# Gram pieces taken out of the fused attention block, chunks given earliest times, and a new written-out order, in a gated-feed-forward kernel with a recurrent attention in front

## The chip, the cores and the metric

One core of one Trainium2 chip runs the whole program. The metric is device time in microseconds (us), the median of three runs. "PE" is the matrix engine, whose weight loads are listed apart as "PEld"; DVE is the vector engine, ACT the scalar engine, POOL the GpSimd engine, SP the queue that issues the transfers.

## The reference

A recurrent attention with a 48x48 state for each of 4 x 8 heads runs over 768 tokens, and its output goes through a gated feed-forward layer:

```python
for t in range(S):                       # 768 tokens
    kt, vt, bt = (k_n[:, :, t], v[:, :, t], beta[:, :, t, None])
    y[:, :, t] = np.einsum('bhd,bhde->bhe', q[:, :, t], state)
    v_old = np.einsum('bhde,bhd->bhe', state, kt)
    state = state + bt[:, :, :, None] * np.einsum('bhd,bhe->bhde', kt, vt - v_old)
...
x = y.transpose(0, 2, 1, 3).reshape(3072, 384)
out = ((x @ w_a) * (x @ w_b)) @ w_out    # w_a, w_b: 384 x 1536, w_out: 1536 x 384
```

## The kernel before

**Attention.** The 768 tokens are cut into 24 chunks of 32, and the chunks into six groups of four (`GROUPS`). Inside a chunk the recurrence is a small triangular system. For each group, `prep(g)` makes the Gram products of its four chunks (keys with keys and keys with queries, one PE piece a chunk) and DVE multiplies them by beta and a mask; `solve(g)` inverts the triangular systems by forward steps on DVE, 31 pairs of instructions for groups 2 to 5. Then `steps(g)` goes through the chunks in order, each with these PE pieces: **Yk** (keys and queries times the state, 32 calls), **U** (the solved update, 32 calls), **S** (the state gets the update, 32 calls, into the bank `S_ps`), **out** (the chunk's own part of the output, 32 calls). A piece of 32 small fp32 calls is issued without a break. From group 2 on (`more`), the **Gram** piece of the next group's chunk, S and out were one block of 96 calls, under one `plan.group()`.

**Feed-forward.** Two chunks make 128 x 2 rows of x, a "sub" of 256 tokens; there are 12 subs and 12 slices of 128 of the hidden width, so 144 units. A unit (`moe`) has 18 fp16 matmuls of 256 columns (here **D**, two runs of nine, with the weights `wh` split in a high and a low half), an ACT copy, a DVE product, an ACT cast, a DVE difference, and two units later (`LAG`) six matmuls of 384 columns with `wo` (here **O**, two runs of three). A unit of a sub needs the outputs of both its chunks.

**What sets the order.** All instructions are recorded first (`Plan.add`), and a planner writes the order of every engine down: `order()` runs `pack()` forward and backward over the recorded pieces. `pack()` is a list scheduler with a table of durations (`price`), delays between engines (`late`), six PSUM banks, a model of PE's clock, and `fetch()`, which counts PE instructions in blocks of 256 and puts a piece later when its block would not be there yet. `boost()` and `BOOST` add urgency by stream. Before, `order()` made up to six rounds (`PASSES`) and kept the one whose planned end was earliest. Until 60 us (`UNTIL`) the planner fills PE's idle time with dummy matmuls on a tile of ones (printed with the line of `issue()`, here 477), so that the clock stays up. At run time nothing of the planned times is left: each engine goes through its list in order and waits for semaphores.

The names `b_3_71` and `xn` are the transposed inverse of a group; `at`, `tt`, `f`, `u` are the small operands of out, U, U and S; `sh` is the copy of the state for Yk; `ghl` is the operand of O. All calls are issued from one helper line, 486.

Of the kernel before, what the change touches and what calls it, by code (L numbers as in the profile page):

```python
# [26 lines left out]
P = 128  # L27
KR = 112
GROUPS = [list(range(i, i + 4)) for i in range(0, NCH, 4)]
NG = len(GROUPS)  # L30
# [5 lines left out]
BOOST = {"first": 9e4, "prep0": 9e4, "solve0": 9e4, "steps0": 9e4, "w0": 7e4, "w1": 7e4, "w2": 6e4, "w3": 6e4, "w4": 6e4, "w5": 6e4, "prep1": 4e4, "solve1": 4e4, "steps1": 4e4, "moe": 1e5}  # L36
# [10 lines left out]
LAG = 2  # L47
LEAD = 4
# [3 lines left out]
class Op:  # L52
    __slots__ = ("eng", "calls", "dur", "move", "rd", "wr", "deps", "pri", "at", "end", "tag", "stream", "banks", "cold", "use", "words")

    def __init__(self, eng):
        self.eng, self.calls, self.dur, self.move = eng, [], 0.0, 0.0
        self.cold, self.use, self.words = 0.0, 0.0, 0
        self.rd, self.wr, self.deps, self.tag, self.banks = {}, {}, set(), "", set()


class Plan:
# [6 lines left out]
    def __init__(self, nc):  # L68
        self.nc = nc
        self.ops = []  # L70
        self.open = None
        self.stream = "first"
        self.masks = {}
        self.pool = []
        self.lease = {}
        self.leases = 0
        self.behind = set()

# [114 lines left out]
    def add(self, eng, fn, name, args, kw):  # L193
# [3 lines left out]
        if self.open is not None and self.open and self.open[-1].eng == eng:  # L197
            op = self.open[-1]
        else:
            op = Op(eng)  # L200
            kind = self.stream + ("_pe" if self.stream == "moe" and eng == "PE" else "")
            op.pri = len(self.ops) - URGENCY.get(kind, URGENCY.get(kind.rstrip("0123456789"), 0))
            op.deps, self.behind = self.behind, set()
            self.ops.append(op)
            op.tag, op.stream = name, self.stream
            if self.open is not None:
                self.open.append(op)
# [63 lines left out]
    def pack(self, pri, back=False):  # L271
# [10 lines left out]
        pos, come = self.BEGIN, [0.0, 0.0]  # L282
        kept = 0 if back else 1
# [5 lines left out]
        while len(done) < n:  # L289
# [23 lines left out]
            while can[e] and i is None:  # L313
                i = heapq.heappop(can[e])[1]
                if ops[i].words and not back:
                    slip = self.fetch(t, ops[i].words, ops[i].dur if warm else ops[i].cold, pos, come, dma)[0]
                    if slip > 1.0:
                        slow.setdefault(i, t)
                        heapq.heappush(wait[e], (t + slip, i))
                        i = None  # L320
                        continue
                need = [] if back else [b for b in ops[i].banks if b not in held]
                if need:
                    at_ = sorted((self.clear(ends, i), k) for k, ends in vacant)
                    if len(at_) < len(need):
                        blocked.append(i)
                        i = None
                    elif at_[len(need) - 1][0] > t:
                        heapq.heappush(wait[e], (at_[len(need) - 1][0], i))
                        i = None  # L330
                    else:
                        for b, (_, k) in zip(need, at_):
                            held[b] = [k, self.users[b], {}]
                        vacant = [x for x in vacant if x[0] not in {k for _, k in at_[: len(need)]}]
# [14 lines left out]
            if e == "PE" and not back:  # L349

                if kept:
# [12 lines left out]
                    while True:  # L364
# [9 lines left out]
                        fill[i][k] += 1  # L374
                _, pos, come = self.fetch(t, o.words, o.dur if warm else o.cold, pos, come, dma)
# [29 lines left out]
            for k, late in nxt[i]:  # L405
                ready[k] = max(ready[k], end + late)
                left[k] -= 1
                if not left[k]:
                    heapq.heappush(wait[ops[k].eng], (ready[k], k))
# [3 lines left out]
    LOADED = (3500.0, 4300.0)  # L413
# [17 lines left out]
    PASSES = 6  # L431

    def order(self):
# [16 lines left out]
        pri, best = [o.pri - boost(o) - 1e12 * (o.stream == 'load') for o in ops], None  # L450
        for _ in range(self.PASSES):
            found = self.pack(pri)
            if found is None:
                break
            at, stop, done, total, bind = found
            if best is None or total < best[0]:
                best = (total, at, stop, done, bind)
            _, stop, _, total, _ = self.pack([-t for t in stop], True)
            pri = [k - 1e12 if o.stream == 'load' else total - t - boost(o) for k, (o, t) in enumerate(zip(ops, stop))]
        for o, o.at, o.end in zip(ops, best[1], best[2]):  # L460
            pass
        self.bind, self.fill = best[4]
        return best[3]
# [26 lines left out]
def tile_kernel(ctx, tc, kqt, kn, vn, begin, w, out):  # L490
# [176 lines left out]
    def tok(h4):  # L667
        return slice(32 * h4, 32 * h4 + 32)
# [26 lines left out]

    def target(c, what):
# [21 lines left out]

    grams, rest = {}, []

    def gram(c):
        rw = raw(c)
        ga = grams[c] = att()
        plan.behind = set(ready if c > 3 else ())
        with plan.group():
            gram_mm(c)
        return ga

    def gram_mm(c):
        rw = raw(c)  # L730
        ga = grams[c].rearrange("p (q n) -> p q n", n=64)
        for q, h4, a, _ in heads():
            T.matmul(
                ga[tok(h4), q, :],
                rw[feat(h4), a, h4 % 2],
                pair(rw[feat(h4), a], h4 % 2),
                start=True,
                stop=True,
                skip_group_check=True,
            )  # L740

    def grammed(g, ci):
        c = GROUPS[g][ci]
        gnat, dc = gnats[g], dcs[g]
        ga = grams[c].rearrange("p (q n) -> p q n", n=64)
        if HALVES[g]:
            kks[c] = ttr()
            A.copy(kks[c], ga[:, :, 0:32])
        V.tensor_mul(
            gnat.rearrange("p k u -> p u k")[:, ci * 8 : ci * 8 + 8, :],  # L750
            ga[:, :, 0:32],
            dc[:, ci * 8 : ci * 8 + 8].unsqueeze(2).broadcast_to([P, 8, 32]),
        )
        ats[c] = atr()
        mask = partial(V.tensor_mul, ats[c], ga[:, :, 32:64], amask.unsqueeze(1).broadcast_to([P, 8, 32]))
        if c == 3:
            rest[:] = mask, {ga.tensor.name: plan.lease[ga.tensor.name]}
        else:
            mask()

    def prep(g):
# [25 lines left out]
        ready.append(len(plan.ops) - 1)  # L787
        gnat = b4().rearrange("p (a b) -> p a b", b=32)
        gnats[g] = gnat
        yield  # L790
        for ci, c in enumerate(chs):
            if g < 3:
                gram(c)
                grammed(g, ci)
            yield
# [125 lines left out]
    def steps(g):  # L921

        chs = GROUPS[g]
        for ci, c in enumerate(chs):
# [5 lines left out]
            else:  # L930
                sh = shr()
                A.copy(sh, S_ps[0:KR, :, 0:384])
                yp = [att(), att()]
                with plan.group():
# [29 lines left out]
            more = g > 1 and g + 1 < NG  # L964
            if more:
                nxt = GROUPS[g + 1][ci]
                grams[nxt] = att()
                lent = {grams[nxt].tensor.name: plan.lease[grams[nxt].tensor.name]}

            def update():  # L970
                for q, h4, a, cols in heads():
                    T.matmul(
                        S_ps[feat(h4), h4 // 2, cols],
                        k2[tok(h4), cols],
                        u[tok(h4), cols],
                        start=(first and q == 0),
                        stop=True,
                        skip_group_check=True,
                    )

            def output():
# [9 lines left out]

            if more:
                plan.behind = set(ready)
                with plan.group():
                    gram_mm(nxt)
                    update()
                    plan.lease.update(mine)
                    output()
            else:
                if not last:  # L1000
                    with plan.group():
                        update()
                plan.lease.update(mine)
                plan.behind = set() if last else {len(plan.ops) - 1}
                with plan.group():
                    output()
# [7 lines left out]
            if more:  # L1014
                plan.lease.update(lent)
                grammed(g + 1, ci)
# [156 lines left out]
    for g in range(1, NG):  # L1173
        n = len(GROUPS[g])
        if g < 2:
            merge((st[g], 3 * n), (moes, 4 * n), (pr[g + 1], 2 + len(GROUPS[g + 1])))
        elif g + 1 < NG:
            next(pr[g + 1])
            merge((st[g], 3 * n), (moes, 4 * n))
            merge((pr[g + 1], 2 + len(GROUPS[g + 1])), (moes, 2))  # L1180
        else:
            merge((st[g], 3 * n), (moes, 4 * n))
# [78 lines left out]
```

## Time and profile before

| what | value |
|---|---|
| median of 3 runs | 658.29 us (657.62 to 666.13) |
| profiled execution, device time | 656.6 us |
| its span, first to last instruction | 654.8 us |
| mean granted PE clock | 0.978 |
| PE busy | 625.1 us, 12208 matmuls |
| DVE busy | 405.0 us |
| ACT busy | 271.6 us |
| POOL busy | 46.0 us |
| transfers | 42.8 MB, mean 65 GB/s |

The device time is 1.8 us more than the span. A busy PE here means that a matmul is in flight: matmuls overlap, so the time that a piece costs is read from its start to the start of the next one. "issue" as the cause of a wait means that nothing which the profile shows (no semaphore, no transfer of data) held the engine back.

### The profile page before, as it was taken

Reading aid. Unit: us, or ns where it says so; the run is one execution under the profiler, and the core shown is the slowest. Engines: PE = TensorE matmul, PEld = TensorE weight load, DVE = VectorE, ACT = ScalarE, POOL = GpSimd, SP = SyncE. Lnnn points to the kernel's source line nnn. Section 1 sums busy time; section 2 is a strip of 40 time slices with the busy share of each in tenths; the row PEclk is TensorE's granted clock in tenths of the full one; section 3 lists DMA queues with packets and bytes.
Section 4 is the critical chain, followed back from the end, with each engine's and each line's share of the span. In section 5 each row is a group of like instructions: output and inputs, shape, how many; then the busy total and the mean of one; then the engine's idle time right before and its main releaser. Section 6 shows DMA issues by size and latency. Waiting matters only on the chain.

```text
span 654.8 us, 26975 instructions
## 1 busy us (share of the span) xinstructions
PE 625.1 (95%) x12208; PEld 534.1 (82%) x12208; DVE 405.0 (62%) x1059; ACT 271.6 (41%) x599; POOL 46.0 (7%) x134
## 2 busy tenths in 40 slices
PE   7998999899999999999989999989999999999997
PEld 6765888678888887888877788877788888888886
DVE  4976888679766994448964368844588442232222
ACT  3455763445534355332372223644224343232322
POOL 0111110111012110000020000100000000000000
PEclk7958999899999999999999999999999999999999
DMA  8655431342255300034000141000000000000000
GB/s 308 175 148 160 137 97 33 96 128 76 77 183 148 97 26 4 21 96 143 0 28 20 43 139 58 1 5 28 3 3 25 4 4 26 1 25 1 25 1 24
DMA packets 20754, 42.80 MB, mean 65 GB/s; under 512 B 2208, under 2 KB 5280, under 8 KB 20640
## 3 DMA queue, kind: packets, MB, share of 16 engines
q1 hardware_dynamic: 20640, 41.08, 20.6%
q8 instruction: 95, 1.56, 1.0%
q14 instruction: 19, 0.16, 0.1%
HBM read 36.36 MB, written 4.72 MB: 63 GB/s over the span
## 4 chain that ended last, share of the span: by engine, by line
PE 87%; DVE 6%; issue 4%; ACT 2%; DMA 1%; SPq 0%; DVEq 0%; ACTq 0%
PE bank L486 83%; PE S_ps L486 3%; DVE b L486 1%; DVE wh L486 1%; DVE tmp L486 1%; DMA rawb<-in_kqt 1%; ACT sqf L486 0%; PE bank L477 0%; DVE late L486 0%; ACT wh L486 0%; DVE ghl L486 0%; DVE f L486 0%; ACT tt L486 0%; DVE g L486 0%; ACT a L486 0%
## 5 line engine op out<-in xcount | busy, mean ns | idle before, releaser
L486 PEld LDWEIGHTS <-wh 128*128 128x128 f16 x2592 | 241.6, 98 | 53.0 <-issue 22.8
L486 PE MATMUL bank<-xb,wh 128*128 128x256 f16 x2160 | 259.5, 273 | 4.3 <-issue 2.7
L486 PE MATMUL bank<-wo,ghl 128*128 128x384 f32 x864 | 191.0, 354 | 0.1
L486 PEld LDWEIGHTS bank<-wo,ghl 128*128 128x128 f32 x864 | 144.7, 190 | 4.4 <-DVE ghl L486 0.5
L486 ACT COPY a<-bank 128x256 f32<-128x256 f32 x144 | 53.5, 372 | 210.8 <-PE bank L486 210.3
L486 DVE TENSOR_TENSOR g<-bank,a 128x256 f32<-128x256 f32 x144 | 61.0, 423 | 127.0 <-ACT a L486 124.0
L486 DVE TENSOR_TENSOR ghl<-g,ghl 128x256 fp32r<-128x256 f32 x144 | 62.1, 431 | 34.0 <-ACT ghl L486 31.9
L486 ACT CAST ghl<-g 128x256 fp32r<-128x256 f32 x144 | 58.1, 404 | 53.6 <-DVE g L486 52.7
L486 DVE TENSOR_TENSOR tmp<-b,b 128x31 f32<-128x31 f32 (+20 forms) x154 | 50.3, 327 | 3.2
L486 PE MATMUL bank<-late,wh 128*128 128x256 f16 x432 | 51.9, 273 | 0.0
L486 DVE TENSOR_TENSOR b<-b,tmp 128x31 f32<-128x31 f32 (+20 forms) x154 | 49.7, 323 | 3.3
L486 PE MATMUL bank<-u,at 32*32 32x48 f32 x1536 | 23.6, 203 | 10.1 <-issue 10.1
L486 PEld LDWEIGHTS bank<-u,at 32*32 32x32 f32 x1536 | 19.1, 105 | 15.1 <-issue 14.2
L486 DVE SCALAR_TENSOR_TENSOR y<-bank,sc,y 128x384 f32<-128x384 f32 x23 | 14.2, 616 | 25.1 <-ACT y L486 24.9
L486 ACT COPY sh<-S_ps 112x768 f32<-112x768 f32 x23 | 18.3, 798 | 22.9 <-PE S_ps L486 22.8
L486 PEld LDWEIGHTS bank<-rawb 48*32 48x32 f32 x1280 | 20.4, 114 | 7.7 <-issue 4.0
L486 PE MATMUL bank<-rawb 48*32 48x64 f32 x1280 | 23.2, 228 | 3.3 <-DMA rawb<-in_kqt 2.4
L486 PEld LDWEIGHTS bank<-sh,rawb 48*64 48x64 f32 x1216 | 19.7, 136 | 5.1 <-issue 3.4
L486 DVE TENSOR_TENSOR b<-bank,dc 128x256 f32<-128x256 f32 x24 | 14.3, 600 | 14.2 <-PE bank L486 13.5
L486 PEld LDWEIGHTS bank<-f,tt 32*32 32x32 f32 x1472 | 17.2, 105 | 6.5 <-issue 3.0
L486 PE MATMUL bank<-sh,rawb 48*64 48x48 f32 x1216 | 22.1, 222 | 0.0
L486 DVE TENSOR_TENSOR f<-vnb,bank 128x384 f32<-128x384 f32 x38 | 19.9, 549 | 3.1 <-PE bank L486 3.1
(123 smaller groups left out, 576.1 us busy)
## 6 DMA issues: line engine op xcount, KB each, us to landing
late<-in_w SPq DMA_DIRECT2D x40, 288.0 KB, 3.0
rawb<-in_kqt SPq DMA_DIRECT2D x32, 256.0 KB, 2.9
out<-late SPq DMA_DIRECT2D x24, 192.0 KB, 1.9
vnb<-in_vn SPq DMA_DIRECT2D x10, 384.0 KB, 3.6
kb<-in_kn SPq DMA_DIRECT2D x9, 384.0 KB, 3.5
wh<-in_w SPq DMA_DIRECT2D x8, 288.0 KB, 3.0
rawb<-in_kqt SPq DMA_DIRECT2D x2, 1024.0 KB, 7.1
late<-in_kqt SPq DMA_DIRECT2D x8, 256.0 KB, 2.7
```

What stands on the lines that cost most here:

```text
L486: fn(*(self.place(a, lease) for a in args), **{k: self.place(a, lease) for k, a in kw.items()})
```

## The change

Five things change.

1. The Gram piece of groups 3, 4 and 5 leaves the fused block. It is issued from `prep(g)`, as it was for groups 0 to 2, as a piece of its own; S and out are two pieces of 32 calls instead of parts of one of 96.
2. An operation can carry an earliest planned time (`hold`). The Yk piece of chunk c from 8 on gets 190 us + (c - 8) x 23 us; the Gram pieces get a time below zero, which holds nothing.
3. `fetch()` is asked three times after 60 us, with the count of PE instructions as planned and 14 fewer and more, and the latest answer counts. The two durations of a block's load go from 3500 and 4300 ns to 3700 and 4400.
4. The priorities come from one round and a fixed list of 38 random changes to them (`jitter`), and the forward pass is made once with the result.
5. The order in which the pieces are recorded for groups 2 to 5 changes (`merge`).

```diff
-    PASSES = 6
+    PASS = 1
+    SEEDS = (100008, 100012, 100025, ..., 103652)
...
+PACE = (190e3, 23e3)
+GRAM = (-1e6, 0)
...
+    LOADED = (3700.0, 4400.0)
+    SHIFTS = (-14, 14)
...
-                    slip = self.fetch(t, ops[i].words, ops[i].dur if warm else ops[i].cold, pos, come, dma)[0]
+                    slip = max(
+                        self.fetch(t, ops[i].words, ops[i].dur if warm else ops[i].cold, p, c, dma)[0]
+                        for p, c in [(pos, come)] + (more if t > self.UNTIL else [])
+                    )
...
-                    heapq.heappush(wait[ops[k].eng], (ready[k], k))
+                    heapq.heappush(wait[ops[k].eng], (max(ready[k], 0.0 if back else ops[k].hold), k))
...
+        for seed in self.SEEDS:
+            pri = jitter(pri, ops, seed)
+        best = self.pack(pri)
...
     def prep(g):
...
         for ci, c in enumerate(chs):
-            if g < 3:
-                gram(c)
-                grammed(g, ci)
+            rw = raw(c)
+            ga = att().rearrange("p (q n) -> p q n", n=64)
+            plan.behind = set(ready[-1:] if g > 2 else ready if g else ())
+            if g > 2:
+                plan.hold = pace(4 * g - 4) + GRAM[0] + ci * GRAM[1]
+            with plan.group():
+                for q, h4, a, _ in heads():
+                    T.matmul(ga[tok(h4), q, :], ...)
...
     def steps(g):
...
                 yp = [att(), att()]
+                if c > 7:
+                    plan.hold = pace(c)
                 with plan.group():
...
-            if more:
-                plan.behind = set(ready)
-                with plan.group():
-                    gram_mm(nxt)
-                    update()
-                    plan.lease.update(mine)
-                    output()
-            else:
-                if not last:
-                    with plan.group():
-                        update()
-                plan.lease.update(mine)
-                plan.behind = set() if last else {len(plan.ops) - 1}
-                with plan.group():
-                    output()
+            if not last:
+                with plan.group():
+                    for q, h4, a, cols in heads():
+                        T.matmul(S_ps[feat(h4), h4 // 2, cols], ...)
+            plan.lease.update(mine)
+            plan.behind = set() if last else {len(plan.ops) - 1}
+            with plan.group():
+                for q, h4, a, cols in heads():
+                    T.matmul(yp[h4 % 2][tok(h4 ^ 1), cols], ...)
...
-            next(pr[g + 1])
-            merge((st[g], 3 * n), (moes, 4 * n))
-            merge((pr[g + 1], 2 + len(GROUPS[g + 1])), (moes, 2))
+        todo = [(st[g], 4 * n), (moes, 4 * n)]
+        if g + 1 < NG:
+            todo.append((pr[g + 1], 2 + len(GROUPS[g + 1])))
+        merge(*todo)
```

What it moves is seen in the written-out order. First PE, at chunk 8, the first with a fused block. `rawb 32x64 x32` is the Gram piece, `S_ps<-u_74,kb` is S, the rows that alternate two banks with `u_74,at_77` are out, `xb,wh` is D. Before:

```order
L486 LDWEIGHTS wh
L486 MATMUL bank_64<-xb,wh 128x256
L486 MATMUL bank_66<-rawb 32x64 x32
L486 MATMUL S_ps<-u_74,kb 48x48 x32
L486 MATMUL bank_65<-u_74,at_77 32x48
L486 MATMUL bank_63<-u_74,at_77 32x48
```

The same place in the changed kernel:

```order
L515 MATMUL bank_65<-wo,ghl_100 128x384 x3
L515 MATMUL S_ps<-u_74,kb 48x48 x32
L515 LDWEIGHTS wh
L515 MATMUL bank_61<-xb,wh 128x256
...
L515 MATMUL bank_66<-rawb 32x64 x32
L515 MATMUL bank_63<-u_74,at_77 32x48
L515 MATMUL bank_64<-u_74,at_77 32x48
```

S now stands ahead of nine D matmuls, and the Gram piece and out behind them; at the other chunks of groups 2 to 4 the three pieces are parted in other ways.

Second PE, where the small products of group 1's solution begin (`tt_85` and `tt_86 32x16`, with `kb 128x256` and `xn 16x16` behind them). Before:

```order
L486 MATMUL bank_66<-wo,ghl_100 128x384 x3
L486 MATMUL bank_64<-b_3_71,tt_85 32x16 x32
L486 MATMUL bank_62<-b_3_71,tt_86 32x16 x32
L486 MATMUL bank_64<-b_3_71,kb 128x256
L486 MATMUL bank_64<-wr_93,xn 16x16 x32
L486 MATMUL bank_62<-b_3_71,kb 128x256
L486 MATMUL bank_63<-wo,ghl_98 128x384 x3
```

In the changed kernel:

```order
L515 MATMUL bank_62<-b_3_71,tt_85 32x16 x32
L515 LDWEIGHTS wh
L515 MATMUL bank_66<-xb,wh 128x256
...
L515 MATMUL bank_62<-b_3_71,kb 128x256
L515 MATMUL bank_62<-wr_93,xn 16x16 x32
L515 MATMUL bank_61<-wo,ghl_100 128x384 x3
L515 MATMUL bank_63<-wo,ghl_100 128x384 x3
L515 MATMUL bank_66<-b_3_71,tt_86 32x16 x32
```

Nine D matmuls now lie behind the first of these products, and O behind the next ones. From here to the Yk piece of chunk 4 there were two units of D before, and there are five now.

Third DVE, at the end of group 0's solve, where PE waits for the transposes. Before:

```order
L486 TENSOR_TENSOR b_2_70<-b_2_70,tmp 128x2x15
L486 STREAM_TRANSPOSE xn<-b_2_70 128x512
L486 STREAM_TRANSPOSE b_3_71<-b_2_70 128x1024
L486 TENSOR_TENSOR sc_127<-sc_127 128x1 x2
L486 TENSOR_TENSOR vnb<-vnb,nm_124 128x384 x2
```

In the changed kernel:

```order
L515 TENSOR_TENSOR b_2_70<-b_2_70,tmp 128x2x15
L515 STREAM_TRANSPOSE b_3_71<-b_2_70 128x1024
L515 STREAM_TRANSPOSE xn<-b_2_70 128x512
L515 TENSOR_TENSOR sc_127<-sc_127 128x1 x2
L515 TENSOR_TENSOR vnb<-vnb,nm_124 128x384 x2
```

The two transposes change places. On every engine the set of instructions is the same but for the dummy matmuls, 36 instead of 38.

More of the change, by code (lines that the diff above doesn't have):

```diff
@@ L1 @@
 import heapq
+import random
 from contextlib import ExitStack
@@ L35 @@
 PARTS = [[i] for i in range(12)]
-BOOST = {"first": 9e4, "prep0": 9e4, "solve0": 9e4, "steps0": 9e4, "w0": 7e4, "w1": 7e4, "w2": 6e4, "w3": 6e4, "w4": 6e4, "w5": 6e4, "prep1": 4e4, "solve1": 4e4, "steps1": 4e4, "moe": 1e5}
+BOOST = {"first": 9e4, "prep0": 9e4, "solve0": 9e4, "steps0": 9e4, "w0": 7e4, "w1": 7e4, "w2": 6e4, "w3": 6e4, "w4": 6e4, "w5": 6e4, "prep1": 4e4, "solve1": 4e4, "steps1": 4e4, "moe": 1e5, "prep2": 0, "solve2": 0, "prep3": 0, "solve3": 0, "prep4": 0, "solve4": 0, "prep5": 0, "solve5": 0}
 LOWS = 4
@@ L52, with jitter @@
 class Op:
-    __slots__ = ("eng", "calls", "dur", "move", "rd", "wr", "deps", "pri", "at", "end", "tag", "stream", "banks", "cold", "use", "words")
+    __slots__ = ("eng", "calls", "dur", "move", "rd", "wr", "deps", "pri", "at", "end", "tag", "stream", "banks", "cold", "use", "words", "hold")
     def __init__(self, eng):
         self.eng, self.calls, self.dur, self.move = eng, [], 0.0, 0.0
-        self.cold, self.use, self.words = 0.0, 0.0, 0
+        self.cold, self.use, self.words, self.hold = 0.0, 0.0, 0, 0.0
         self.rd, self.wr, self.deps, self.tag, self.banks = {}, {}, set(), "", set()
+def jitter(pri, ops, seed):
+    r = random.Random(seed)
+    kind, amp = r.randrange(3), r.choice((500.0, 3000.0, 10000.0, 30000.0))
+    names = sorted({o.stream for o in ops})
+    name, start = r.choice(names), r.randrange(len(ops))
+    move, new = r.gauss(0.0, amp), []
+    for i, (o, p) in enumerate(zip(ops, pri)):
+        u, g = r.random(), r.gauss(0.0, amp)
+        if o.stream != "load":
+            if kind == 0 and u < 0.03:
+                p += g
+            elif kind == 1 and o.stream == name:
+                p += move
+            elif kind == 2 and start <= i < start + 200:
+                p += g
+        new.append(p)
+    return new
 class Plan:
@@ L77, in __init__ @@
         self.behind = set()
+        self.hold = 0.0
     def bank(self, kind, n):
@@ L203, in add @@
             op.deps, self.behind = self.behind, set()
+            op.hold, self.hold = self.hold, 0.0
             self.ops.append(op)
@@ L282, in pack @@
         pos, come = self.BEGIN, [0.0, 0.0]
+        more = [(self.BEGIN + d, [0.0, 0.0]) for d in self.SHIFTS]
         kept = 0 if back else 1
@@ L374, in pack @@
                         fill[i][k] += 1
+                words = o.words + sum(a * b for a, b in zip(fill.get(i, (0, 0)), (2, 4)))
+                more = [self.fetch(t, words, o.dur if warm else o.cold, p, c, dma)[1:] for p, c in more]
                 _, pos, come = self.fetch(t, o.words, o.dur if warm else o.cold, pos, come, dma)
@@ L408, in pack @@
                 if not left[k]:
-                    heapq.heappush(wait[ops[k].eng], (ready[k], k))
+                    heapq.heappush(wait[ops[k].eng], (max(ready[k], 0.0 if back else ops[k].hold), k))
         return at, stop, done, max(stop), ({b: h[0] for b, h in held.items()}, fill)
     MOVE = (1200.0, 1300.0)
-    LOADED = (3500.0, 4300.0)
+    LOADED = (3700.0, 4400.0)
+    SHIFTS = (-14, 14)
     BEGIN, IDLE, SINCE, UNTIL = 63, (50.0, 440.0), 1200.0, 60e3
@@ L430 @@
     WINDOW = 3413.0
-    PASSES = 6
+    PASS = 1
+    SEEDS = (100008, 100012, 100025, 100028, 100036, 100060, 100080, 100120, 100128, 100156, 100186, 100218, 100234, 100242, 100544, 101409, 101448, 101457, 101467, 101488, 101638, 101762, 101769, 101798, 101976, 101998, 102133, 102140, 102164, 102398, 102610, 103130, 103197, 103230, 103254, 103258, 103359, 103652)
     def order(self):
@@ L449, in order @@
                 self.pred[i].append((j, late))
-        pri, best = [o.pri - boost(o) - 1e12 * (o.stream == 'load') for o in ops], None
-        for _ in range(self.PASSES):
+        pri = [o.pri - boost(o) - 1e12 * (o.stream == "load") for o in ops]
+        for _ in range(self.PASS):
             found = self.pack(pri)
[L453 to L457, printed above, removed]
+            stop = found[1] if found else [float(k) for k in range(len(ops))]
             _, stop, _, total, _ = self.pack([-t for t in stop], True)
-            pri = [k - 1e12 if o.stream == 'load' else total - t - boost(o) for k, (o, t) in enumerate(zip(ops, stop))]
-        for o, o.at, o.end in zip(ops, best[1], best[2]):
-            pass
+            pri = [k - 1e12 if o.stream == "load" else total - t - boost(o) for k, (o, t) in enumerate(zip(ops, stop))]
+        for seed in self.SEEDS:
+            pri = jitter(pri, ops, seed)
+        best = self.pack(pri)
         self.bind, self.fill = best[4]
-        return best[3]
+        return best[2]
     def place(self, x, lease):
@@ L694, in pieces, with pace @@
         return [(dst[:, i], src[:, i]) for i in range(dst.shape[1])]
+    def pace(c):
+        return PACE[0] + (c - 8) * PACE[1]
     def target(c, what):
@@ L717, in load @@
             SP.dma_start(rawp(c).rearrange("p c (h d) -> p (c h) d", h=2), kqt[c // 2][:, :, 0:512])
[L719 to L724, printed above, removed]
-        with plan.group():
[L726 to L757, printed above, removed]
-        else:
-            mask()
     def prep(g):
@@ L787, in prep @@
         ready.append(len(plan.ops) - 1)
+        yield
         gnat = b4().rearrange("p (a b) -> p a b", b=32)
         gnats[g] = gnat
-        yield
         for ci, c in enumerate(chs):
-            if g < 3:
-                gram(c)
-                grammed(g, ci)
+            rw = raw(c)
[5 more added lines that the diff above has]
+                for q, h4, a, _ in heads():
+                    T.matmul(
+                        ga[tok(h4), q, :],
+                        rw[feat(h4), a, h4 % 2],
+                        pair(rw[feat(h4), a], h4 % 2),
+                        start=True,
+                        stop=True,
+                        skip_group_check=True,
+                    )
+            if HALVES[g]:
+                kks[c] = ttr()
+                A.copy(kks[c], ga[:, :, 0:32])
+            V.tensor_mul(
+                gnat.rearrange("p k u -> p u k")[:, ci * 8 : ci * 8 + 8, :],
+                ga[:, :, 0:32],
+                dc[:, ci * 8 : ci * 8 + 8].unsqueeze(2).broadcast_to([P, 8, 32]),
+            )
+            ats[c] = atr()
+            if c == 3:
+                rest = partial(V.tensor_mul, ats[c], ga[:, :, 32:64], amask.unsqueeze(1).broadcast_to([P, 8, 32]))
+                rest = rest, {t.tensor.name: plan.lease[t.tensor.name] for t in [ga]}
+            else:
+                V.tensor_mul(ats[c], ga[:, :, 32:64], amask.unsqueeze(1).broadcast_to([P, 8, 32]))
             yield
@@ L962, in steps @@
             yield
-            more = g > 1 and g + 1 < NG
-            if more:
[L966 to L981, printed above, removed]
+            if not last:
+                with plan.group():
+                    for q, h4, a, cols in heads():
+                        T.matmul(
+                            S_ps[feat(h4), h4 // 2, cols],
+                            k2[tok(h4), cols],
+                            u[tok(h4), cols],
+                            start=(first and q == 0),
+                            stop=True,
+                            skip_group_check=True,
+                        )
+            plan.lease.update(mine)
+            plan.behind = set() if last else {len(plan.ops) - 1}
+            with plan.group():
                 for q, h4, a, cols in heads():
@@ L990, in output @@
                     )
-            if more:
-                plan.behind = set(ready)
-                with plan.group():
-                    gram_mm(nxt)
-                    update()
-                    plan.lease.update(mine)
-                    output()
-            else:
-                if not last:
-                    with plan.group():
-                        update()
-                plan.lease.update(mine)
-                plan.behind = set() if last else {len(plan.ops) - 1}
-                with plan.group():
-                    output()
             y32 = yr()
@@ L1013, in steps @@
                 V.scalar_tensor_tensor(y32, yp[1][:, 0:384], zeo[:, 0:1], y32, op0=ALU.mult, op1=ALU.add)
-            if more:
-                plan.lease.update(lent)
-                grammed(g + 1, ci)
             yT = ytr()
@@ L1174, in tile_kernel @@
         n = len(GROUPS[g])
-        if g < 2:
-            merge((st[g], 3 * n), (moes, 4 * n), (pr[g + 1], 2 + len(GROUPS[g + 1])))
-        elif g + 1 < NG:
-            next(pr[g + 1])
-            merge((st[g], 3 * n), (moes, 4 * n))
-            merge((pr[g + 1], 2 + len(GROUPS[g + 1])), (moes, 2))
-        else:
-            merge((st[g], 3 * n), (moes, 4 * n))
+        todo = [(st[g], 4 * n), (moes, 4 * n)]
+        if g + 1 < NG:
+            todo.append((pr[g + 1], 2 + len(GROUPS[g + 1])))
+        merge(*todo)
         queue.extend((s, list(range(NFC))) for s in range(GROUPS[g][0] // 2, GROUPS[g][-1] // 2 + 1))
```

## The prediction

> **What bounds the kernel now.** I read the page first, its busy time and its chain.
>
> ```profile
> PE 625.1 (95%) x12208; PEld 534.1 (82%) x12208; DVE 405.0 (62%) x1059; ACT 271.6 (41%) x599; POOL 46.0 (7%) x134
> PE 87%; DVE 6%; issue 4%; ACT 2%; DMA 1%; SPq 0%; DVEq 0%; ACTq 0%
> q8 instruction: 95, 1.56, 1.0%
> ```
>
> PE bounds it: it is busy for 95% and is 87% of the chain. The change alters no product, so it can only win what PE loses between and beside its matmuls. The second share to look at is "issue", 4% or some 26 us, time in which nothing visible held the engine. The third row is a hint: 95 packets with 1.56 MB are 16.4 KB each, and the 24416 matmuls and weight loads of the first row make 95 times 257. So PE's instructions arrive in blocks of about 256.
>
> Next I asked what PE waited for.
>
> ```profile
> PE bank L486 <- issue: 17.3, 18, 1.7
> PE bank L486 <- DMA rawb<-in_kqt: 2.4, 1, 2.4
> PE bank L486 <- DVE sc L486: 1.3, 1, 1.3
> PE S_ps L486 <- issue: 1.3, 1, 1.3
> ```
>
> 19 waits of "issue" hold 18.6 us; every other cause is below 2.5. Then the timeline of PE shows where they lie. Its columns are start, length, instruction, and in brackets the idle time before it; two neighbouring starts give the cost of a piece.
>
> ```profile
> 248.93 0.93 PE L486 MATMUL S_ps<-u,kb 32*48 32x48 f32 x63
> 251.13 0.20 PE L486 MATMUL S_ps<-u,kb 32*48 32x48 f32 x1 [1.27 <-issue]
> 251.26 0.88 PE L486 MATMUL bank<-u,at 32*32 32x48 f32 x64
> 252.07 1.16 PE L486 MATMUL bank<-xb,wh 128*128 128x256 f16 x9
> 252.98 1.30 PE L486 MATMUL bank<-wo,ghl 128*128 128x384 f32 x6
> 254.12 2.14 PE L486 MATMUL bank<-xb,wh 128*128 128x256 f16 x18
> 256.19 1.15 PE L486 MATMUL bank<-sh,rawb 48*64 48x48 f32 x64
> 257.27 1.32 PE L486 MATMUL bank<-wo,ghl 128*128 128x384 f32 x6
> 258.43 1.16 PE L486 MATMUL bank<-xb,wh 128*128 128x256 f16 x9
> 259.51 0.88 PE L486 MATMUL bank<-f,tt 32*32 32x48 f32 x64
> 260.33 1.16 PE L486 MATMUL bank<-xb,wh 128*128 128x256 f16 x9
> 261.42 1.10 PE L486 MATMUL bank<-rawb 48*32 48x64 f32 x64
> 262.44 0.93 PE L486 MATMUL S_ps<-u,kb 32*48 32x48 f32 x64
> 263.31 0.27 PE L486 MATMUL bank<-u,at 32*32 32x48 f32 x5
> 264.38 0.87 PE L486 MATMUL bank<-u,at 32*32 32x48 f32 x59 [0.80 <-issue]
> ```
>
> Both waits fall into the middle of a piece: one call short of the end of S, then after 5 matmuls of out. Nothing in the program asks for a wait there. Count what lies between them: 1+64+9+6+18+64+6+9+64+9+64+64+5 = 383 matmuls, each with its weight load, so 766 instructions, and two or three semaphore instructions make it 768, three times 256. Over the whole trace I counted likewise: 15 waits behind the first D all stand at instruction 256k+193, and one "issue" wait (335.94 us) does not. So the cause is the next block of instructions. The block that ended at 264.38 had begun 133 matmuls earlier, with Gram at 261.42: 256 instructions in 2.96 us with the wait. Over the 15 waits this spacing of two block ends is 2.4 to 3.8 us, 3.05 in the mean. **A stretch of PE that issues 256 instructions in less than about 3.05 us waits for the rest.** A D run needs 18 instructions for 1.09 us (260.33 to 261.42) and never does; the fused block issues 384 in 2.7 us and often does.
>
> These waits price themselves. S takes 0.87 us at 262.44 and 2.33 at 248.93, so 1.27 idle costs 1.46; 0.80 idle likewise costs 1.0: 0.2 more than the row says, since the matmul before it still counts as busy.
>
> ```profile
> 35.47 0.62 PE L486 MATMUL bank<-wr,xn 32*16 32x16 f32 x52 [0.37 <-issue]
> 39.25 1.40 PE L486 MATMUL bank<-vnb,tt 32*32 32x48 f32 x57 [0.38 <-issue]
> 50.98 0.23 PE L486 MATMUL bank<-b,tt 32*32 32x16 f32 x2 [1.70 <-issue]
> 119.84 0.24 PE L486 MATMUL bank<-wr,xn 32*16 32x16 f32 x6 [1.12 <-issue]
> 335.94 1.10 PE L486 MATMUL bank<-rawb 48*32 48x64 f32 x64 [0.91 <-issue]
> 467.72 1.05 PE L486 MATMUL bank<-xb,wh 128*128 128x256 f16 x8 [1.24 <-issue]
> ```
>
> Three rows lie ahead of the first D (2.45 us idle, about 3 with the 0.2 each). From the first (119.84) to the last (467.72) there are 18.6 - 2.45 - 0.91 = 15.2 us in 15 waits, with 15 x 0.2 **18.3 us**.
>
> **The change part by part.** The sum is made against the profiled execution, 656.6 us; the timed median is 1.7 above it and the lowest timed run 1.0.
>
> *Blocks of instructions.* I walked along PE's order of both kernels: 4 instructions a small fp32 call, 2 a D or O, one for a second semaphore, each piece by the starts above (Yk 1.08 us, U and out 0.81, S 0.86, Gram 1.03, D 0.99 a nine, O 0.19 each), and charged what two block ends lay closer than 3.05 us. For the kernel before it gives 18.5 us behind the first D, against 18.3 measured, and 14 of its 15 places are those of the trace, so the walk may be used. For the changed order it gives **5.3 us** in nine places, none above 1.2: S, Gram and out no longer make 384 instructions in a row. That is **-13.0**. With 2.4 us for a block it is 8.8 to 1.2, with 3.8 it is 32.5 to 15.8; with the count 32 instructions later it is 14.0 instead of 5.3, 32 earlier 0.8. So the ends are -17.5 and -4. Ahead of the first D the walk gives 3.5 instead of 5.4; scaled to the 3 measured, **-1.0**.
>
> The Trainium skill speaks against this: "Runtime: NRT & Kernel Launch", section "Instruction fetch mechanics", says that blocks of 256 instructions are fetched ahead and that crossing a boundary is mostly hidden. The block size agrees with the 16.4 KB packets; hidden it is not, by the 1.27 us row. By the page this term would be 0 and the sum 656.4.
>
> *More borders of pieces.* D x9 costs 1.09 us before a small piece (260.33), 0.91 before O (252.07), and 0.98 ahead of nine others (2.07 - 1.09 at 254.12). Likewise O:
>
> ```profile
> 244.66 0.78 PE L486 MATMUL bank<-wo,ghl 128*128 128x384 f32 x3
> 245.37 0.88 PE L486 MATMUL bank<-f,tt 32*32 32x48 f32 x64
> 246.18 0.79 PE L486 MATMUL bank<-wo,ghl 128*128 128x384 f32 x3
> 246.81 1.16 PE L486 MATMUL bank<-xb,wh 128*128 128x256 f16 x9
> ```
>
> Three O cost 0.71 us before a small piece and 0.63 before D. The order has 58 borders from D to small pieces (50 before), 31 from O to small (25), and 88 from D to O (107). That is 8 x 0.09 + 6 x 0.08 + 19 x 0.08 = **+2.7**. These are the borders that splitting makes; behind a small piece I find no extra (0.81 for out before D, 0.86 for S before out).
>
> *Head.* PE's dummies end when the first transpose of group 0 that it needs is done:
>
> ```profile
> 28.50 1.07 DVE L486 STREAM_TRANSPOSE xn<-b 128x512 f32<-128x512 f32 x1
> 29.49 1.20 DVE L486 STREAM_TRANSPOSE b<-b 128x1024 f32<-128x1024 f32 x1
> 30.84 1.29 PE L486 MATMUL bank<-b,tt 32*32 32x16 f32 x128 [1.29 <-DVE sc L486]
> ```
>
> Changing places gives PE its operand at 28.50 + 1.2 instead of 29.49 + 1.2: **-1.0**, the same as the two dummies less (0.43 each). xn is read later, behind a product and an ACT step, so it should not be missed; if it were, the gain would be 0.
>
> *Middle.* Rows of the stretches (length, then busy time of PE, PEld, DVE, ACT, POOL, then PE's clock and the transfers):
>
> ```profile
> 30.84:71.81 40.97, 37.73 (x1274) 26.27 (x1274) 31.50 (x72) 22.52 (x48) 8.48 (x21) 0.79 0.53 149
> 115.78:139.98 24.20, 21.67 (x714) 16.92 (x713) 17.73 (x31) 12.34 (x29) 3.90 (x10) 0.93 0.43 125
> 295.34:333.73 38.39, 38.39 (x359) 34.07 (x360) 33.55 (x102) 16.38 (x39) 5.07 (x10) 1.00 0.20 57
> ```
>
> Between the first products of group 1 and the Yk of chunk 4 the pieces add up to 18.0 us by the prices above, and took 24.2. Two block waits are 2.5 of the 6.2; the other 3.7 are small waits for ACT and DVE and a stretch of half clock (0.93 in the mean). The new order puts five units of D there instead of two, which cover such waits. I take half, **-2**, between 0 and -3.7.
>
> *New waits.* Moved with the pieces are the DVE products behind Gram, ACT's copies, and on SP two stores that now stand ahead of input loads; POOL's scalings of v shift by a place or two. PE waited for a transfer once, 2.4 us at the start, so I cost these at 0, covered by D and O; a load that came too late would cost 2 to 3. The solves are the tight place: U of the next group stands in PE's list about where DVE is done, and DVE is busy for 33.55 of 38.39 us. Adding the same prices, the distance from a group's last Gram to its first U goes from 40.2, 43.6, 41.6, 39.6 us to 37.8, 43.2, 42.0, 38.5 for groups 2 to 5, and DVE's instructions in between from 102, 102, 93, 91 to 90, 90, 103, 91. Groups 2 and 3 lose more DVE work than time, group 4 gains 10 small ones, group 5 loses 1.1 us of cover. I take **+1.5**, between 0 and +6 (1.5 a group).
>
> **Sum**: -13.0 - 1.0 + 2.7 - 1.0 - 2 + 1.5 = -12.8, so 643.8 for a profiled execution, **644** in the timed runs, 1.95% less. Two per cent (13 us) is about what a measurement of this kernel can tell from no change, so the forecast lies on that border.
>
> **The rivals.**
>
> *The order is too tight for DVE.* Then U waits, and with it all of D behind it. At 2 us in each of four groups and 1.5 in the chunks the term is +9.5 instead of +1.5: 652. For it: 33.55 of 38.39. Against it: before, PE lost nothing there (38.39 busy of 38.39).
>
> *The waits are not blocks but drains* between pieces of different shape. By it they stay, 18.3 us, and the borders come on top: 656.6 + 2.7 - 3 = 656. The waits in the middle of pieces speak against it. The Trainium skill, "TensorEngine Tiling (Array Packing)", "Key Properties", says that a change of the tiling mode drains PE; by the rows this is the 0.09 us at D's border, and no more.
>
> *Slower than before.* The same late solve, but by more: when a solve ends 5 us behind its U, four groups cost 20 instead of the 1.5, and the sum is 662. It decides from 3.6 us a group on, where 4 x 3.6 eats the 12.8 and the 1.5. Group 4's ten more DVE instructions speak for it, but at 0.15 to 0.6 us each they make 3 at most; groups 2 and 3 speak against it.
>
> **How the numbers follow.** Forecast, blocks of instructions mostly gone: 0.76, between 635 and 650 by its own bounds. Order too tight: 0.15. Drains or another cause that stays: 0.05. Slower: 0.04. The range **635 to 652** takes in the forecast and most of the second. Two per cent under 658.3 is 645.1; the forecast's middle lies 1 below, and two thirds of its own range lie below: 0.76 x 0.68 makes **0.52** for faster, **0.45** for within 2%, **0.03** for slower.
>
> **What would show it.** PE's "issue" waits should fall from 18.6 us to below 9, and those left stand again at block ends. S, Gram and out should show no wait inside. The first small product behind the dummies should start near 29.9. The stretch from there to the Yk of chunk 4 should lose under 4 us instead of 6.2. PE should wait for DVE or ACT at the first U of groups 2 to 5 by under 1.5 us each. The forecast is wrong if block ends are closer than counted (many waits of 0.5 to 1 at new places), or if those U rows show a wait.

## The result, and the profile after

The changed kernel takes **636.36 us** in the median of 4 runs (635.39 to 638.85), 0.964 of the kernel before (95% interval 0.956 to 0.971). The profiled execution took 635.4 us, with a span of 633.6: 21.2 us less than the 656.6 of before. The forecast was 644, between 635 and 652, with 12.8 us less in the sum. The direction, the range and the cause hold; the size was too small by 8.4 us. Of the same kernel, run again below as a yardstick, the profiled execution took 1001.75 us at a granted clock of 0.558 and is in none of the ratios given here.

The page of the changed kernel, in the rows that answer to those of before:

```profile
PE 615.6 (97%) x12204; PEld 527.5 (83%) x12204; DVE 405.0 (64%) x1059; ACT 269.0 (42%) x599; POOL 47.7 (8%) x134
PE 77%; DVE 5%; ACT 4%; issue 1%; ACTq 0%
q8 instruction: 95, 1.56, 1.1%
```

DVE has the same 405.0 us, PE four matmul records fewer (the two dummies) and 9.5 us less busy time, and "issue" has shrunk from 4% to 1% in the chain. (This chain can be followed back only to 82 us, so its shares add up to 87%, and those of before to 100%.) The waits by cause are the safer comparison:

```profile
PE bank L515 <- issue: 5.5, 9, 1.3
PE bank L515 <- DMA rawb<-in_kqt: 3.6, 2, 2.8
PE bank L515 <- DVE b L515: 1.3, 1, 1.3
PE bank L515 <- DVE g L515: 0.8, 2, 0.6
```

18.6 us of "issue" in 19 waits have become 5.5 in 9. At chunks 8 and 9, the place that was shown for before, the timeline of PE now reads:

```profile
243.39 0.93 PE L515 MATMUL S_ps<-u,kb 32*48 32x48 f32 x64 [0.24 <-ACT u L515]
244.26 1.16 PE L515 MATMUL bank<-xb,wh 128*128 128x256 f16 x9
245.35 1.10 PE L515 MATMUL bank<-rawb 48*32 48x64 f32 x64
246.37 0.88 PE L515 MATMUL bank<-u,at 32*32 32x48 f32 x64
247.19 1.16 PE L515 MATMUL bank<-xb,wh 128*128 128x256 f16 x9
...
254.53 0.93 PE L515 MATMUL S_ps<-u,kb 32*48 32x48 f32 x64
255.40 2.14 PE L515 MATMUL bank<-xb,wh 128*128 128x256 f16 x18
257.30 0.77 PE L515 MATMUL bank<-wo,ghl 128*128 128x384 f32 x3
258.00 0.88 PE L515 MATMUL bank<-u,at 32*32 32x48 f32 x64
```

The pieces cost what they did (S 0.87 us, Gram 1.02, out 0.82). At these chunks no three of them follow one another, and no block end holds one. Five block waits are left behind the first D, again at instruction 256k+193, one of them under 0.1 us; the longest stands between two O:

```profile
365.64 1.50 PE L515 MATMUL bank<-wo,ghl 128*128 128x384 f32 x7
367.80 0.97 PE L515 MATMUL bank<-wo,ghl 128*128 128x384 f32 x4 [0.65 <-issue]
```

To see where the 21.2 us came from, I set the time at which a piece started against the sum of the prices of all pieces ahead of it (those of the prediction, from neighbouring starts). What is over is lost time:

| up to | before: start, lost | after: start, lost | gain in the stretch |
|---|---|---|---|
| first Gram of group 1 | 89.3, 23.7 | 84.6, 20.4 | 3.3 |
| Yk of chunk 4 | 140.0, 30.5 | 137.1, 23.2 | 4.0 |
| first Gram of group 2 | 195.3, 32.5 | 188.1, 23.7 | 1.5 |
| end of the last matmul | 651.3, 54.0 | 630.1, 30.9 | 14.3 |

The losses shrink by 23.1 us, and the prices themselves rise by 1.9 (599.2 instead of 597.3: more borders, two dummies less); together 21.2.

### The profile page after: what moved, and what is told of

Same layout as the page of the kernel before. It is cut to its first block, busy times and chain, and to the rows that moved or that the text cites. A ratio compares the mean times of both kernels' runs of the same rounds, so it can differ in the third digit from the quotient of the medians.

```text
span 633.6 us, 26978 instructions
## 1 busy us (share of the span) xinstructions
PE 615.6 (97%) x12204; PEld 527.5 (83%) x12204; DVE 405.0 (64%) x1059; ACT 269.0 (42%) x599; POOL 47.7 (8%) x134
## 4 chain that ended last, share of the span: by engine, by line
PE 77%; DVE 5%; ACT 4%; issue 1%; ACTq 0%
PE bank L515 74%; PE S_ps L515 3%; DVE b L515 2%; ACT sqf L515 1%; DVE tmp L515 1%; ACT tt L515 1%; DVE g L515 1%; ACT ghl L515 1%; DVE ghl L515 1%; ACT a L515 0%; DVE at L515 0%; DVE s L515 0%; DVE f L515 0%; DVE ss L515 0%; DVE sc L515 0%
## 5 line engine op out<-in xcount | busy, mean ns | idle before, releaser
L515 PE MATMUL bank<-wo,ghl 128*128 128x384 f32 x864 | 187.7, 352 | 1.2 <-issue 1.1
L515 PE MATMUL bank<-rawb 48*32 48x64 f32 x1280 | 21.2, 217 | 5.2 <-DMA rawb<-in_kqt 3.6
L515 PEld LDWEIGHTS bank<-rawb 48*32 48x32 f32 x1280 | 18.7, 107 | 8.8 <-issue 4.8
L515 POOL COPY late<-late 1x1 int32<-1x1 int32 x44 | 13.1, 302 | 118.9 <-DMA late<-in_w 49.1
L515 ACT ACTIVATE sqf<-rawb 48x1024 bf16<-48x1024 f32 x20 | 21.1, 1056 | 0.4
L515 PE MATMUL bank<-u,at 32*32 32x48 f32 x1536 | 21.2, 202 | 0.0
```

The costliest lines, as they stand in the source:

```text
L515: fn(*(self.place(a, lease) for a in args), **{k: self.place(a, lease) for k, a in kw.items()})
```

## The experiments

**Theory**: PE's "issue" waits are ends of blocks of 256 instructions that come too soon after one another. **Rival**: they belong to borders between pieces of different shape, or to the length of the fused block as such. The two are told apart by moving the block ends without touching the order.

The trace of before also holds the transfers themselves. Its instruction queue, q8, has 95 packets, and behind the first block end they pair off with the block ends in order. All 15 waits behind the first D end 1.30 to 1.51 us after their own packet has landed: the packet of the wait that ends at 251.13 runs from 248.69 to 249.62 us, that of 264.38 from 262.04 to 262.96. No block end of that trace is passed sooner than 1.28 us after its packet. So these waits are waits for a block of the program; the runs below show what they cost.

### The same orders with the block ends moved

The changed kernel once more, as the yardstick on the same chip:

> The changed kernel once more, as the yardstick of the three shifted kernels on the same chip. Expected 635 to 639 us, PE's block waits behind the first D about 2.6 us, at the same instructions as in its first profile (all at 256k+193).

It took 635.41 us in the median, 0.965 of before (0.961 to 0.969); before took 657.80 us in this set of runs. Whether its block waits stand where they stood is left open.

Next the **kernel before** with 64 tiny matmuls at its start, which move all later block ends by half a block:

```diff
+    EXTRA = (40, 0, 24)   # tiny dummies ahead of the first, second, third filled piece
...
-            for i in self.order():
+            done = self.order()
+            for i, n in zip([i for i in done if any(self.fill.get(i, ()))], self.EXTRA):
+                self.fill[i][0] += n
+            for i in done:
```

> The kernel before with 64 tiny dummy matmuls (128 instructions) put into PE's idle time at the start, 40 ahead of the first Gram piece and 24 ahead of the first small product; every other instruction and its order stay. Blocks theory: all later block ends move by half a block, the walk along the order gives 5.6 us of waits behind the first D instead of 18.5, so about 13 us less: 641 to 647 in a profile. Drains theory (waits belong to borders between pieces of different shape): the borders are the same, so the waits stay at 18 us and the time at 656 to 660.

642.33 us, 0.976 of before (0.972 to 0.980), the profiled one 641.7. The fused blocks are all still there. Its waits for "issue", and its timeline at chunk 9, where the kernel before waited in the middle of out:

```profile
PE bank L491 <- issue: 8.5, 10, 1.5
```

```profile
260.20 1.10 PE L491 MATMUL bank<-rawb 48*32 48x64 f32 x64
261.23 1.07 PE L491 MATMUL S_ps<-u,kb 32*48 32x48 f32 x64
262.23 0.88 PE L491 MATMUL bank<-u,at 32*32 32x48 f32 x64
263.04 1.14 PE L491 MATMUL bank<-wo,ghl 128*128 128x384 f32 x5
265.11 0.33 PE L491 MATMUL bank<-wo,ghl 128*128 128x384 f32 x1 [0.93 <-issue]
```

Gram, S and out run through, 384 instructions in 2.84 us, and the wait comes five O later, where the next block ends. At chunk 8 a wait of 1.45 us is left, one call short of the end of out (250.73 us); at the other chunks it is gone. Behind the first D the block waits are 4.3 us (four rows with 3.5 us idle, and 0.2 each) instead of 18.3; the walk had said 5.6. From the first Gram of group 2 on it loses 8.0 us, before 21.5, the changed kernel 7.2. There the clock is 1.00 in both kernels, so the higher mean clock of this run (0.989 instead of 0.978, a matter of the start) is no part of these 13.5 us. So the rival falls: same borders, same blocks of 96 calls, and the waits have gone with the block ends.

Then the other way round: the **changed kernel** with 16 tiny matmuls more at its start, by the same edit.

```diff
+    EXTRA = (16,)
```

> The changed kernel with 16 tiny dummy matmuls (32 instructions) at its start, all else in the same order. Blocks theory: the walk gives 14.0 us of waits with 3.05 us for a block and 8.6 with 2.75, instead of 5.3 and 2.9: 5 to 9 us slower than the changed kernel, 641 to 646. Drains theory: no change, within 1 us.

645.02 us, 0.979 of before (0.975 to 0.983) and 9.6 above the yardstick, at the upper end of what was expected. The block waits behind the first D are 9.2 us (nine rows with 7.4 us idle) instead of 2.6; some stand inside S and Gram:

```profile
98.92 0.21 PE L520 MATMUL bank<-rawb 48*32 48x64 f32 x1 [1.73 <-issue]
...
374.12 0.84 PE L520 MATMUL S_ps<-u,kb 32*48 32x48 f32 x55
376.29 0.33 PE L520 MATMUL S_ps<-u,kb 32*48 32x48 f32 x9 [1.33 <-issue]
```

That is 6.6 of the 9.6 us. Up to the first Gram of group 1 it loses 25.3 us instead of 20.4, and only 1.2 of these 4.9 are such a wait. Ahead of the first D the block waits are hardly longer, 3.9 us idle instead of 3.4; what differs there is the clock, 0.89 in the mean up to the first Gram of group 1 instead of 0.94. Whether the moved block ends brought that about, or the one profiled execution, is not shown. 32 instructions of 24400, in time that PE had to spare, take back almost half of what the change won.

And 32 instructions fewer, by wider dummies:

```diff
-                for k, n in enumerate(self.fill.get(i, ())):
+                small, big = self.fill.get(i, (0, 0))
+                wide = 8 if big > 16 else 0
+                for k, n in (0, small), (1, big - 2 * wide), (2, wide):   # 2: 512 columns
```

> The changed kernel with 16 of the 26 dummy matmuls of 256 columns ahead of the first small product replaced by 8 of 512 columns: the same dummy time with 32 instructions fewer. Blocks theory: the walk gives 0.2 to 0.8 us of waits instead of 2.9 to 5.3, so 1.5 to 2.5 us faster than the changed kernel. Drains theory: no change.

634.93 us, 0.5 below the yardstick and so the same; the waits behind the first D fell only from 2.6 to 1.7 us. Most of it is one wait, longer than all that the walk gave together:

```profile
342.79 0.62 PE L517 MATMUL bank<-wo,ghl 128*128 128x384 f32 x2
344.40 1.49 PE L517 MATMUL bank<-wo,ghl 128*128 128x384 f32 x7 [0.99 <-issue]
```

The expectation of 1.5 to 2.5 us was too high. It is the fastest median of all, but not clear of the changed kernel.

### The parts of the change

The changed program planned as before: single pieces, but neither earliest times nor the triple count nor the random changes.

```diff
-        for seed in self.SEEDS:
-            pri = jitter(pri, ops, seed)
-        best = self.pack(pri)
+        for _ in range(self.PASSES):      # the loop of before, 6 rounds, best kept
...
-    LOADED = (3700.0, 4400.0)
-    SHIFTS = (-14, 14)
+    LOADED = (3500.0, 4300.0)
+    SHIFTS = ()
...
-                if c > 7:
-                    plan.hold = pace(c)
```

> The changed program (Gram, S and out as single pieces, recorded in the new order), but planned as before: six rounds, no random changes, no earliest times, one count of instructions, the old two durations of a block. Theory 1 (breaking the block of 96 calls is what counts): the walk along its order gives 6.5 us of block waits behind the first D instead of 18.5, and the pieces add up to 1.4 us more, so 643 to 647, the part from chunk 8 on as fast as in the changed kernel. Theory 2 (the order search made the gain): near 655.

643.88 us, 0.977 of before (0.973 to 0.982; before took 660.35 us in this set of runs). The parted pieces with their new order of recording, which were not taken apart, bring some 15 us, as much as moving the block ends alone, and theory 2 falls. Behind chunk 8's Gram (the first of group 2) it loses 9.3 us, ahead of it 30.2.

The changed kernel without the random changes:

```diff
-    SEEDS = (100008, 100012, 100025, ..., 103652)
+    SEEDS = ()
```

> The changed kernel without the 38 random changes of the priorities, all else kept. The walk gives 7.7 us of block waits instead of 5.3, and the pieces add up to 2.1 us less than in the changed kernel. Theory 1 (the blocks are all): 635 to 638. Theory 2 (the search also brought the 8.8 us that the first 190 us lost less than before): 643 to 647, with the loss ahead of chunk 8's Gram near 31 us instead of 23.7.

638.61 us, 0.969 of before (0.964 to 0.973), between the two theories. It loses 28.5 us up to chunk 8's Gram, against 23.7 of the changed kernel: more, though not the 31 of theory 2, and its pieces cost 2.1 us less. Its block waits are 3.1 us where the walk had 7.7. The windows from 105 to 145 us (length, busy time of PE, PEld, DVE, ACT, POOL, PE's clock) show a part of the difference; first without the random changes, then the changed kernel:

```profile
105.00:145.00 40.00, 37.44 (x1033) 30.51 (x1036) 31.46 (x64) 17.45 (x40) 5.24 (x12) 0.87 0.33 92
```

```profile
105.00:145.00 40.00, 39.84 (x1095) 32.71 (x1093) 33.93 (x66) 20.23 (x46) 5.28 (x16) 1.00 0.37 112
```

PE is idle for 2.6 us instead of 0.2, and 10.2 us run at half clock, none with the random changes.

The same without the earliest times:

```diff
-                if c > 7:
-                    plan.hold = pace(c)
```

> As the run without random changes, and also without the earliest times of the Yk pieces. If spreading the chunks matters by itself, it is slower by several us than with them (the walk: 9.4 us of block waits against 7.7, the pieces equal, so 1 to 2 us); if only the parting of the pieces matters, no difference.

640.57 us against 638.61, 0.971 of before (0.967 to 0.976): 2 us for spreading the chunks, though the two intervals overlap. The number is the one forecast, but not for the reason given: the walk put it on block waits, 9.4 us against 7.7, and they measure 3.2 against 3.1. What the 2 us are is open.

Last the random changes kept and the earliest times left out:

> The changed kernel with its random changes but without the earliest times of the Yk pieces. The walk gives 5.9 us of block waits against 5.3, and the pieces add up to 0.4 us less: within 2 us of the changed kernel if the block waits decide behind chunk 8; but the random list was made for another order, so the first 190 us may lose what it won there, up to 9 us.

665.6 us, **1.009 of before** (1.006 to 1.012), within 2% of it but slower than every other program here. Of the 30 us above the changed kernel a single wait makes 22.7:

```profile
PE bank L515 <- DVE at L515: 22.7, 1, 22.7
PE bank L515 <- issue: 4.7, 7, 1.5
```

```profile
238.96 2.29 PE L515 MATMUL bank<-xb,wh 128*128 128x256 f16 x10 [22.65 <-DVE at L515]
```

```profile
215.00:245.00 30.00, 7.35 (x37) 5.27 (x36) 27.07 (x80) 7.13 (x15) 3.36 (x5) 0.60 0.07 22
```

```profile
236.27 0.19 DVE L515 TENSOR_TENSOR b<-b,tmp 128x31 f32<-128x31 f32 x1
236.50 1.25 DVE L515 STREAM_TRANSPOSE b<-b 128x1024 f32<-128x1024 f32 x1
237.67 0.91 DVE L515 TENSOR_REDUCE ss<-sqf 128x16 f32<-128x768 f32 x1
238.50 0.41 DVE L515 TENSOR_TENSOR at<-bank,kb 128x256 f32<-128x256 f32 x1
```

PE stands still while DVE goes through group 2's solve (27.07 of 30 us busy), and the clock reads 0.60 there. The product `at`, for which D waits, stands behind the whole solve in DVE's list. It is no operand of D; by the rows, what D waits for is the PSUM bank that this product reads. Even the slower side of the expectation, 9 us more, was short by some 21 us: I looked only at the walk along PE, and it cannot see such a wait. The block waits are lower than forecast (2.5 us behind the first D instead of 5.9). The other 7 us or so above the changed kernel are not explained. The list of random changes was picked for one program, and here it did not carry over to another.

## Why the prediction was right, and where it was off

**The main cause was right.** The walk along PE's order with 3.05 us a block, made from the trace of before alone, ranked the two orders and their shifts as measured. Walk, then measured (waits of 0.2 us and more, with 0.2 added to each), in us behind the first D: before 18.5, 18.3; before moved by 128 5.6, 4.3; changed 5.3, 2.6; changed moved by 32 14.0, 9.2; changed moved by -32 0.8, 1.7. It did not rank the four programs that were planned anew: parted pieces only 6.5, 4.9; without random changes 7.7, 3.1; without these and the earliest times 9.4, 3.2; without the earliest times 5.9, 2.5. So it tells 18 us from 3, but not 9 from 6. By the Trainium skill's "Runtime: NRT & Kernel Launch", section "Instruction fetch mechanics", crossing a block is mostly hidden; the term that would then be 0 measured 15.7 us here.

**Terms of the sum**, forecast and measured:

| stretch | forecast | measured |
|---|---|---|
| prices of all pieces (borders, dummies) | +1.7 | +1.9 |
| up to the first Gram of group 1 | -1.0 | -3.3 |
| to the Yk of chunk 4 (its block waits with it) | -4.0 | -4.0 |
| to the first Gram of group 2 | 0 | -1.5 |
| to the end, block waits | -11.0 | -13.2 |
| to the end, other waits | +1.5 | -1.1 |
| sum | -12.8 | -21.2 |

*Blocks of instructions.* Behind the first D mis-sized by 2.7 us: the walk leaves 5.3, the chip 2.6. The mean of 3.05 came from block ends that did wait; with 2.75 the walk gives 2.9. Ahead of the first D the term had the wrong sign: forecast was 1.0 us less, and the waits there rose from 2.45 us idle in three to 3.40 in four, at 15.60, 33.73, 37.50 and 58.57 us. The gain of that stretch came in spite of it. *New waits*, 1.5 us for a solve that ends too late, did not come: U of chunks 12, 16 and 20 starts in the changed kernel without a wait for DVE, and other waits fell by 1.1. That was the largest error for which the trace had spoken against me, with PE 38.39 of 38.39 us busy. *Head.* The transposes did change places as said:

```profile
27.92 1.25 DVE L515 STREAM_TRANSPOSE b<-b 128x1024 f32<-128x1024 f32 x1
29.09 1.00 DVE L515 STREAM_TRANSPOSE xn<-b 128x512 f32<-128x512 f32 x1
```

```profile
29.32 0.86 PE L515 MATMUL bank<-b,tt 32*32 32x16 f32 x82 [1.32 <-DVE b L515]
```

The first product starts at 29.32 instead of 30.84, and 29.9 was expected: DVE reached its transposes 0.58 us earlier as well (27.92 instead of 28.50). What I left out is the clock. From the first product on it reads, before, 0.79 over 40.97 us up to the first D and 1.00 over the 43.97 us behind it; in the changed kernel, up to the end of chunk 3 (first row):

```profile
29.32:80.10 50.78, 46.91 (x1547) 34.96 (x1547) 41.13 (x98) 31.39 (x67) 10.64 (x26) 0.90 0.54 156
107.80:137.10 29.30, 29.30 (x848) 23.78 (x848) 23.43 (x46) 15.68 (x35) 3.60 (x12) 1.00 0.41 125
```

The clock in the records is either full or half, so 0.21 x 2 x 41 is 17 us at half clock, 0.10 x 2 x 51 is 10. Taken from the start, the means up to the first Gram of group 1 are 0.87 over 89.27 us and 0.94 over 84.57, or 23 us at half clock against 10. These 13 us cost what PE's work in them takes longer; that they make up the 2.3 us that the forecast lacks there is argued, not shown. Part of it may be luck of the profiled execution: its clock is 0.991, and the other three timed runs of the changed kernel have 0.984 to 0.988 and take up to 3.5 us more. *Middle.* The second row is the stretch that I expected to lose under 4 us: PE is busy in all 29.30 us of it at full clock, and it lost at most 2.8.

*Slips in the working.* The block that ended at 264.38 had begun 128 matmuls earlier, not 133, five matmuls into Gram at 261.50; its spacing is 2.88 us instead of 2.96. Without the block term of 13.0 the sum is 656.8, not 656.4. Ten DVE instructions of 0.15 to 0.6 us make up to 6 us, not 3 at most. And since the timed median of before lay 1.7 above its profiled execution, 643.8 for a profiled execution goes with 645.5 for timed runs, not 644. None of them changes the direction.

**The rivals.** Drains fell by the moved block ends. An order too tight for DVE, the case of the slower side, is not what the changed kernel met, but it is real: without the earliest times the same list of random changes makes 22.7 us of it, though at a D and not at the U that the rival named.

**What the change consists of**, by the runs: parting the pieces and the new order of recording some 15 us, the new planning without random changes and holds some 3 (one round, the triple count and the longer load times, not taken apart), the earliest times 2, the random changes 2 to 3. The last two lie within overlapping intervals and are not clear of the noise. These are medians of different program orders, and each moves the block ends of everything behind it, so the shares hold for this sequence alone.

## What to carry to other kernels

When the profile shows an engine waiting for "issue" in the middle of a piece, count its instructions between such waits; a multiple of 256, as here on PE, speaks for a wait for its program, and packets on the instruction queue that land shortly before each restart confirm it. Then look for stretches that issue a block faster than one arrives, part them with work that needs few instructions for its time, and try the cheapest edit first: a few dummy instructions in idle time, which here brought 15 us, against some 22 for the whole change, without moving anything. Any later edit that adds or removes instructions moves all block ends behind it, so a gain of a per cent in such a kernel is to be measured beside the same kernel with its count shifted.

## What was unexpected of the hardware

Two block ends on PE need not lie 3 us apart: in the trace of before one follows the last by 2.05 us without a wait (528.08 us), another by 2.88 with one (264.38), and one by 5.08 and waits all the same (295.34). The packets tell them apart: the first had begun 0.32 us ahead of the block end before it, the second 0.54 behind it, the third 2.64 behind it, and PE goes on 1.3 to 1.5 us after the landing in each. So a spacing is only the mean of a spread, and the walk is off where a fetch starts early or late; why one starts when it does is open. And 32 instructions, 0.13% of PE's program, moved the time by 9.6 us.
